# A gated linear attention and a spatial-gating MLP on one core: units in another order, and shifted due times for 66 steps beside TensorE

## The chip, the cores and the metric

The kernel runs on one core of one Trainium2 chip. The metric is the device time of one execution in microseconds (us). The kernel before took 347.85 us (median of 3 runs, 346.72 to 348.61). Engines: PE is TensorE (matmuls), PEld its weight loads, DVE VectorE, ACT ScalarE, POOL GpSimd; SP issues the DMAs.

## What is computed

Cut to what matters:

```python
# attention: batch 4, 8 heads, 768 steps, head dimension 48
for t in range(S):
    state = alpha[:, :, t, :, None] * state + einsum('bhd,bhe->bhde', k[:, :, t], v[:, :, t])
    y[:, :, t] = einsum('bhd,bhde->bhe', q[:, :, t], state)
x = y.transpose(0, 2, 1, 3).reshape(B, S, H * D)          # (4, 768, 384)
# MLP with a spatial gate
h = gelu(x @ w_in)                                         # 384 -> 1024
u, v = h[..., :512], h[..., 512:]
v_n = (v - mean) / sqrt(var + 1e-6) * g_ln
v_s = einsum('ts,bsd->btd', w_sg, v_n) + b_sg[None, :, None]
out = x + (u * v_s) @ w_out
```

## The kernel before

**Chunks.** The recurrence is cut into 24 chunks of 128 steps, six for each of the four batches, numbered 0 to 23. A scan on DVE (line 415) makes the running product of the decays of a chunk, a second scan (437) its inverse; k and q are scaled with them (428, 444), and the rest of a chunk is small matmuls of 64x64, run two at a time in the two halves of the array ("tiled").

**Units of PE.** The program for PE is a sequence of units, written out by hand in the string `ORDER`. `S i`, `A i`, `M i`, `H i` are the four tiled units of chunk i: scores (line 472), their product with v and the gains of the state (487, 510), the second half of that with the carried state (487, 498), the end (498). `T i` transposes k for the first chunks. `V b c` (mm_v, 9 matmuls of 128x512) and `U b h d` (mm_u, 9 of 128x384) are the products with w_in, `P b h d` (mm_s, 18) the spatial product, `R b h k` (mm_o, 12) that with w_out. `Q g m` (mm_q, 9) are the pieces of the spatial product of the last batch, which is computed with seven products in place of eight from sums of weights and values. Every float32 matmul that needs precision is three matmuls of high and low halves (lines 703 to 705).

**Around a chunk.** `A i` waits for the masked scores (`causal`, DVE, line 581) and for the rows of k (`kn`, ACT, 614 and 618). Between `A i` and `M i` stands `turn`, a tiny write that orders the two halves of a bank: on POOL a memset of `relay`, on ACT a copy of `alo` (line 554). `H i` waits for `half` (633, DVE or ACT). After `H i` ACT copies y out (`xf` 659, `y3` 649), SP packs it with two DMAs (662), ACT rounds it (`xh`, 670), DVE takes the rest (`xl`, 674). `V` needs `xh` and `xl`; its output goes through GELU, moments, the root on POOL (730, 731), the normalisation and again a split into `vh` (ACT 747) and `vl` (DVE 751), which `P` reads in the order of the six chunks.

**Sums of weights.** `weight_sums` (854) makes the four sums of blocks of w_sg for the last batch: six loads of 393 KB, 12 differences (872), 12 roundings on ACT (876), 12 remainders (880), 24 stores to DRAM (883). Its loads may start at the planner's time `SUMS`; 24 `fetch` DMAs (899) bring the sums back later.

**The planner.** Everything on the other engines is a step with an engine, a cost, predecessors and buffers. `Plan.dues` (97) gives each step a due time, worked back from the due times of the units; `Plan.issue` (122) then walks through a modelled time and at each point takes, among the steps of an engine that could start nearly at once, the one with the lowest `order`:

```python
near = [x for x in c if x[0] - left[x[2]]["keen"] <= t0 + (150 if e == "pe" else 60)]
t, way_order, n, way = min(near, key=lambda x: x[1])
```

What it picks is written into the program in that order, so each engine and SP's queue run strictly in it. Where a step has two possible engines, the walk takes the one that would end it first.

**The branch.** Near the end all engines load a count (`cnt_i`, line 1588) and branch (1589): a slow path is skipped when the inputs are in range. A hint for the branch is given to PE alone, behind the last but one `Q` of `ORDER` (`hint_at`, 1122).

Of the kernel before, what the change touches and what calls it, by code (L numbers as in the profile page):

```python
# [48 lines left out]
F64_MIN_AS_F32 = float(np.array(0x38100000, np.uint32).view(np.float32))  # L49

ORDER = """
    T0 A0 H0 S0 A1 S1 M0 T2 T1 S2 T3 H1 V00 S3 V01 M1 H2 M2 A2 S4 U000 A3 M4 H3 U002 M3 T4 A4 S5 T5 A5 V02 S6 M5 H4
    V03 S7 M6 H5 A7 H6 A6 V04 V05 U001 U010 P000 S8 P002 M7 U013 U003 U011 P003 P001 S9 P010 P013 H7 A8 S10 H8 H9 M8
    A9 U012 R000 M9 R001 V11 V10 P012 R002 A10 P011 S11 V12 A11 S12 H10 M11 M10 U100 H11 R011 A12 M12 U103 V13 R012
    P101 P100 V14 R010 V15 U101 P103 U102 H12 S13 P102 U111 U112 R102 U113 S14 U110 M13 S15 A13 H14 H13 A14 P110 M14
    R100 P112 U203 R101 P113 S16 A16 H15 A15 P111 V22 M15 M16 H16 U202 R111 V24 V23 R112 R110 S18 M17 S17 A18 V21 A17
    U200 H17 M18 H18 V20 S19 S20 A19 U201 M20 A20 M19 H19 V25 S21 H20 P200 U210 P202 P210 U211 R202 P203 A21 P201 S22
    R200 P211 P213 R201 H21 M21 V31 S23 A22 H22 U213 M23 V30 M22 H23 A23 P212 V34 U212 V35 V32 U310 U302 U303 Q11 Q12
    R211 Q01 V33 R212 R210 U312 Q02 Q05 U300 U301 U311 Q06 Q04 Q16 Q17 Q15 Q03 Q07 R301 U313 Q13 R310 Q14 R311 C0 R302
    R300 R312  # L60
"""

FIRST = (
    ("a", 0), ("kqv", 0), ("ws", 0), ("ws", 1), ("v", 0), ("a", 1), ("kqv", 1), ("wv", 0), ("v", 1), ("wv", 1),
    ("ws", 2), ("ws", 3), ("ws", 4), ("ws", 5),
)


class Plan:
# [27 lines left out]
    def dues(self):  # L97
        kids = {n: [] for n in self.steps}
        for n, s in self.steps.items():
            for a in s["after"]:  # L100
                kids[a].append(n)
        memo = {}

        def due(n):
            if n in memo:
                return memo[n]
            s = self.steps[n]
            memo[n] = 1e9
            d = s["due"] if s["due"] is not None else 1e9
            if s["soon"] is not None:  # L110
                a, ns = s["soon"]
                d = min(d, due(a) + ns)
            cost = s["ns"] + (s["reach"] or self.REACH[s["eng"]]) + (2200 + round(s["nbytes"] / self.RATE) if s["nbytes"] else 0)
            for k in kids[n]:
                d = min(d, due(k) - cost - self.steps[k]["lead"].get(n, 0))
            memo[n] = d
            return d

        for n in self.steps:
            self.steps[n]["order"] = due(n)  # L120

    def issue(self, units, ahead):
        self.dues()
# [71 lines left out]
def tile_gla_gmlp(ctx: ExitStack, tc: tile.TileContext, aT, kqv, w_in, w_sgT, w_out, g_ln, b_sg, out):  # L195
# [903 lines left out]
    n = B * NCH  # L1099
# [23 lines left out]
    due = {}  # L1123
# [10 lines left out]
    for name, p in pieces:  # L1134
        def at(k, name=name):
            return (k,) + name
# [188 lines left out]
    for b in range(B):  # L1325
        for c in range(NCH):
            summed = b in SUMMED
            st_ = mlp_v(xs.setdefault((b, c // CPH), {}), vns[b][c], c, summed)
            v = ("V", b, c)
# [18 lines left out]
        for hf in range(2):  # L1348
            x = xs[b, hf]
# [52 lines left out]


    LAST = ("V", B - 1, NCH - 1)
    SUMS = 140000.0
    order = (0, 1, 3, 2)
    for k in range(NK):
        load, total, high, low_half, keep = weight_sums(k)
# [5 lines left out]
        for w in range(2):  # L1414
            plan.add(at("load", w), "sp", 330, lambda w=w, load=load: load(w), takes=[("raw", 2, uses[w])], nbytes=393216, start=SUMS)
        for m, (prev, users) in zip(order, ((None, [at("t", 1)]), (0, [at("t", 3)]), (1, []), (3, []))):
# [127 lines left out]
    for k, src in enumerate(words):  # L1544
        t = {}

        def load(src=src, t=t):
            t["raw"] = stage.tile([P, TH, 2], I32, tag="raw", name="raw", bufs=2)
            nc.sync.dma_start(t["raw"], src.bitcast(I32).rearrange("p (n two) -> p n two", two=2))
# [127 lines left out]
```

## Time and profile before

| | before |
|---|---|
| time, median of 3 runs | 347.85 us (346.72 to 348.61) |
| time of the profiled execution | 347.15 us |
| its span, first to last instruction | 345.4 us |
| granted TensorE clock, mean | 0.993 |
| PE busy | 333.7 us, 97% |
| PEld busy | 301.1 us, 87% |
| DVE busy | 264.4 us, 77% |
| ACT busy | 186.8 us, 54% |
| POOL busy | 60.2 us, 17% |

The span is the time between the first and the last instruction on the core; the 1.75 us between it and the execution's own time lie around it. Busy time of PE counts a matmul from its start to its modelled end, and matmuls overlap: what a unit costs is therefore read here from the start of its first matmul to the start of the next unit's first.

### The profile page before, as it was taken

How to read it: one execution, taken by the hardware profiler on the slowest of the kernel's cores; microseconds unless marked ns; L12 is line 12 of the kernel's file. 1: busy time of each engine (PE TensorE's matmuls, PEld its weight loads, DVE VectorE, ACT ScalarE, POOL GpSimd, SP SyncE). 2: the span in 40 equal slices, each digit the busy share in tenths (PEclk: the TensorE clock that was granted, in tenths of full speed). 3: DMA queues.
4: the chain of work that ended last, by engine and by line, in shares of the span. 5: the costliest groups of instructions: out<-in, count | busy, mean ns of one | idle time of the engine just before them, and what ended most of it. 6: DMA issues, size and time to landing. Idle time of an engine off the chain costs nothing. (4 is left out here: it accounts for less than half of the span.)

```text
span 345.4 us, 10871 instructions
## 1 busy us (share of the span) xinstructions
PE 333.7 (97%) x4435; PEld 301.1 (87%) x4435; DVE 264.4 (77%) x547; ACT 186.8 (54%) x462; POOL 60.2 (17%) x145
## 2 busy tenths in 40 slices
PE   8989999899999999999999998998999999999996
PEld 4667888699979988999999986897999899999996
DVE  5999997799998786488679787868655576896752
ACT  4656887988354788545546466759322445241210
POOL 2011313241022324100010034530000124000000
PEclk9999999999999999999999998999999999999999
DMA  7968676658535462646776676897981340010012
GB/s 246 376 203 248 207 181 198 179 122 245 163 103 155 105 183 63 180 149 174 237 184 185 205 207 199 297 267 92 384 272 49 88 137 0 25 46 2 6 58 86
DMA packets 45227, 56.17 MB, mean 163 GB/s; under 512 B 18800, under 2 KB 38384, under 8 KB 45168
## 3 DMA queue, kind: packets, MB, share of 16 engines
q1 hardware_dynamic: 45168, 55.39, 54.1%
q8 instruction: 36, 0.59, 0.7%
q14 instruction: 23, 0.19, 0.2%
HBM read 38.84 MB, written 9.44 MB: 140 GB/s over the span
## 5 line engine op out<-in xcount | busy, mean ns | idle before, releaser
L703 PE MATMUL mm_s<-ws_hi,vh 128*128 128x384 f32 x144 | 48.8, 339 | 0.8 <-ACT vh L747 0.6
L705 PE MATMUL mm_s<-ws_hi,vl 128*128 128x384 f32 x144 | 48.3, 335 | 0.1
L704 PE MATMUL mm_s<-ws_lo,vh 128*128 128x384 f32 x144 | 48.1, 334 | 0.0
L703 PE MATMUL mm_u<-xh,wi_hi 128*128 128x384 f32 x96 | 33.0, 344 | 0.0
L705 PE MATMUL mm_u<-xh,wi_lo 128*128 128x384 f32 x96 | 32.2, 336 | 0.0
L704 PE MATMUL mm_u<-xl,wi_hi 128*128 128x384 f32 x96 | 32.2, 335 | 0.0
L703 PE MATMUL mm_v<-wi_hi,xh 128*128 128x512 f32 x72 | 29.8, 414 | 0.7 <-ACT xh L670 0.7
L840 ACT CAST gh<-g 128x384 fp32r<-128x384 f32 x28 | 14.2, 512 | 27.6 <-DVE g L837 16.1
L704 PE MATMUL mm_v<-wi_lo,xh 128*128 128x512 f32 x72 | 28.7, 399 | 0.0
L705 PE MATMUL mm_v<-wi_hi,xl 128*128 128x512 f32 x72 | 28.7, 399 | 0.0
L703 PEld LDWEIGHTS mm_s<-ws_hi,vh 128*128 128x128 f32 x144 | 27.0, 188 | 1.8 <-ACT vh L747 0.9
L703 PE MATMUL mm_o<-gh,wo_hi 128*128 128x384 f32 x84 | 28.3, 337 | 0.0
L705 PE MATMUL mm_o<-gh,wo_lo 128*128 128x384 f32 x84 | 28.1, 335 | 0.0
L704 PE MATMUL mm_o<-gl,wo_hi 128*128 128x384 f32 x84 | 28.1, 334 | 0.0
L705 PEld LDWEIGHTS mm_s<-ws_hi,vl 128*128 128x128 f32 x144 | 27.0, 188 | 0.4 <-DVE vl L751 0.4
L704 PEld LDWEIGHTS mm_s<-ws_lo,vh 128*128 128x128 f32 x144 | 27.0, 188 | 0.0
L487 PEld LDWEIGHTS y<-at,kqv_t 64*64 64x64 f32 x768 | 16.1, 133 | 11.7 <-issue 5.1
L487 PE MATMUL y<-at,kqv_t 64*64 64x64 f32 x768 | 22.1, 227 | 3.6 <-POOL relay L554 1.3
L415 DVE TENSOR_TENSOR_SCAN pf<-a,floor 128x387 f32<-128x387 f32 x24 | 22.8, 955 | 2.7 <-DMA a<-in_aT 2.5
L614 ACT COPY kn<-kt 128x768 uint16<-128x768 uint16 x18 | 19.2, 1068 | 9.0 <-PE dl L510 5.4
L424 POOL COPY pend<-pf 128x3 f32<-128x3 f32 x24 | 10.1, 421 | 78.3 <-DVE pf L415 70.9
L1004 DVE TENSOR_TENSOR r<-mm_o,xf 128x384 f32<-128x384 f32 x23 | 12.5, 552 | 14.1 <-PE mm_o L705 11.0
(198 smaller groups left out, 876.0 us busy)
## 6 DMA issues: line engine op xcount, KB each, us to landing
kqv_t<-in_kqv SPq DMA_DIRECT2D x22, 586.0 KB, 4.3
a<-in_aT SPq DMA_DIRECT2D x30, 194.0 KB, 3.8
raw<-in_w_in SPq DMA_DIRECT2D x14, 384.0 KB, 4.9
out_x<-r SPq DMA_DIRECT2D x23, 192.0 KB, 2.1
raw<-in_w_out SPq DMA_DIRECT2D x8, 384.0 KB, 4.2
sum_t<-t_dram SPq DMA_DIRECT2D x16, 192.0 KB, 4.6
kqv_t<-kqv_t SPq DMA_DIRECT2D x48, 48.2 KB, 2.9
raw<-in_w_sgT SPq DMA_DIRECT2D x6, 384.0 KB, 4.4
```

Of the source, the lines that this page charges most:

```text
L415: nc.vector.tensor_tensor_scan(pf.rearrange("p j t -> p (j t)"), s["a"][:, 0:NK * C1], floor.rearrange("p j t -> p (j t)"), initial=0.0, o ...
L424: nc.gpsimd.tensor_copy(pend[:, i], st[i]["pf"][:, :, C])
L487: lambda j=j: nc.tensor.matmul(y_of(y, m, j, e)[:, half(h)], v[half(h), D * (2 * j + e):D * (2 * j + e) + 64], at[half(h), e, m, j], start ...
L614: nc.scalar.copy(to[:, 0:2 * NK * P].rearrange("t (k d two) -> t two k d", two=2, k=NK), kt,)
L703: nc.tensor.matmul(o, lh, rh, start=(idx == 0 and not onto), stop=False, skip_group_check=shared)
L704: nc.tensor.matmul(o, lh, rl, start=False, stop=False, skip_group_check=shared)
L705: nc.tensor.matmul(o, ll, rh, start=False, stop=(idx == n - 1), skip_group_check=shared)
L840: nc.scalar.copy(gate_part(g, "h", d), t["g"])
L1004: nc.vector.tensor_tensor(t["r"], t["o"], x["xf"][:, kk], op=ALU.add)
```

## The change

Three things change, and no step is added or taken away. `ORDER` lists the same 221 units in another sequence. A new table `SHIFT` adds an amount in ns to the `order` of 66 steps that are not on PE; the walk then picks those steps earlier or later among their rivals. And `SUMS` goes from 140000 to 95000, so the sums of weights may be loaded earlier. As the lines move down by 15, line 554 is 569 in the changed kernel, 880 is 895, and so on.

```diff
 ORDER = """
-    T0 A0 H0 S0 A1 S1 M0 T2 T1 S2 T3 H1 V00 S3 V01 M1 H2 M2 A2 S4 U000 A3 M4 H3 U002 M3 T4 A4 S5 T5 A5 V02 S6 M5 H4
...
+    M0 S1 T0 S0 A0 H1 M1 T1 A1 H0 T3 V00 S2 T2 S3 V01 A3 A2 M2 H2 S4 U000 U002 A4 H3 M3 S5 T4 M4 A5 T5 H4 V02 V03 A6
...
 """
+SHIFT = """
+    load_wv_1:68663 power_wv_2:-1890 power_wu_2:-12837 load_wu_3:-6539 rest_wu_3:-20747 load_ws_2_0:64246
...
+"""
...
+        shift = {n: int(v) for n, v in (x.split(":") for x in SHIFT.split())}
         for n in self.steps:
-            self.steps[n]["order"] = due(n)
+            self.steps[n]["order"] = due(n) + shift.pop("_".join(map(str, n)), 0)
+        assert not shift, shift
...
-    SUMS = 140000.0
+    SUMS = 95000.0
```

**What it moves on PE.** The sequence written for PE passes between tiled units and full-size ones 58 times before and 52 times in the change. Gone are three islands of tiled units between large ones: `H7 S9`, `H12 S13`, and `S17` between `R112` and `R110`; one is new (`H13 S14`, seven large units behind `M13`). Near the start `S2 T2` now stands behind `M1 H1`, not ahead of them. The last `V` is `V32` where it was `V33`. The hint for the branch stands 73 matmuls ahead of it, where it stood 45 ahead.

**POOL around chunk 17.** The first fence is of before, the second of the change. `rstd` and `off` belong to a unit `V` of batch 2 (moments `mv`), `pend` to the scan of a later chunk, and the memset of `relay` is `turn` of chunk 17, for which `M17` waits.

```order
L730 TENSOR_SCALAR rstd_3482<-mv_3475 128x1
L731 TENSOR_TENSOR rstd_3482<-rstd_3482,nhalf_106 128x1
L735 TENSOR_SCALAR off_3525<-mv_3475,rstd_3482 128x1
L880 TENSOR_TENSOR sum_lo_3529<-sum_w_3349,sum_hi_3480 128x384
L730 TENSOR_SCALAR rstd_3536<-mv_3532 128x1
L731 TENSOR_TENSOR rstd_3536<-rstd_3536,nhalf_106 128x1
L554 MEMSET relay_105 128x1
L735 TENSOR_SCALAR off_3579<-mv_3532,rstd_3536 128x1
```

```order
L745 TENSOR_SCALAR rstd_3442<-mv_3438 128x1
L746 TENSOR_TENSOR rstd_3442<-rstd_3442,nhalf_106 128x1
L750 TENSOR_SCALAR off_3451<-mv_3438,rstd_3442 128x1
L745 TENSOR_SCALAR rstd_3470<-mv_3453 128x1
L746 TENSOR_TENSOR rstd_3470<-rstd_3470,nhalf_106 128x1
L750 TENSOR_SCALAR off_3496<-mv_3453,rstd_3470 128x1
L439 COPY pend_109<-pf_3521 128x3
L569 MEMSET relay_105 128x1
L745 TENSOR_SCALAR rstd_3626<-mv_3614 128x1
```

Before, the root of `V24` (730, 731) and a remainder of the sums (880) stand right ahead of the memset; in the change it stands behind the root and the offset of the earlier `V23` and one copy, the next root comes after it, and the sum is no longer on POOL.

**ACT around chunk 14.** `turn` of chunk 14 was on POOL right behind that of chunk 13. In the change it is the copy of `alo` on ACT:

```order
L891 CAST sum_hi_2947<-sum_w_2871 128x384
L436 COPY kqv_t_2920<-pf_2489 128x3
L619 COPY pi_2534<-kqv_t_2920 128x768
L685 CAST xh_2836<-xf_2621 128x3x128
L819 ACTIVATE u_3025<-mm_u_2977 128x384
L569 COPY alo2_88<-alo_98 128x1
L891 CAST sum_hi_3047<-sum_w_2945 128x384
```

Ahead of it now stand the decay's end and the planes of chunk 17 (436, 619), `xh` of chunk 13 (685), which waits for two DMAs, and the GELU of `U112` (819), the unit right before `A14`.

**DVE ahead of chunk 10.** The first fence is of before, the second of the change; the last row of each is `half` of chunk 10 (`s_m<-s_c,dl0`), for which `H10` waits.

```order
L1004 TENSOR_TENSOR r_1999<-mm_o_1948,xf_393 128x384
L437 SCALAR_TENSOR_TENSOR pi_2003<-a_1633,ends_103 128x387
L415 SCALAR_TENSOR_TENSOR pf_2027<-a_1993,floor_100 128x387
L432 RECIPROCAL ends_103<-pf_2027 128x3
L1004 TENSOR_TENSOR r_2054<-mm_o_2012,xf_393 128x384
L843 TENSOR_TENSOR gl_2056<-g_1713,gh_2052 128x384
L832 SCALAR_TENSOR_TENSOR g_2063<-mm_s_1973,g_col_119,b_bc_120 128x384
L843 TENSOR_TENSOR gl_2056<-g_1764,gh_2052 128x384
L837 TENSOR_TENSOR g_2063<-g_2063,u_1827 128x384
L437 SCALAR_TENSOR_TENSOR pi_2068<-a_1993,ends_103 128x387
L832 SCALAR_TENSOR_TENSOR g_2100<-mm_s_2033,g_col_119,b_bc_120 128x384
L633 TENSOR_TENSOR s_m_111<-s_c_110,dl0_2080 112x192
```

```order
L1019 TENSOR_TENSOR r_2017<-mm_o_1937,xf_401 128x384
L430 SCALAR_TENSOR_TENSOR pf_2022<-a_1984,floor_100 128x387
L895 TENSOR_TENSOR sum_lo_2047<-sum_w_1986,sum_hi_2024 128x384
L447 RECIPROCAL ends_103<-pf_2022 128x3
L887 TENSOR_TENSOR sum_w_2054<-raw_1905,sum_w_1997 128x384
L858 TENSOR_TENSOR gl_2059<-g_1706,gh_2049 128x384
L1019 TENSOR_TENSOR r_2061<-mm_o_2004,xf_401 128x384
L847 SCALAR_TENSOR_TENSOR g_2063<-mm_s_1964,g_col_119,b_bc_120 128x384
L858 TENSOR_TENSOR gl_2059<-g_1774,gh_2049 128x384
L452 SCALAR_TENSOR_TENSOR pi_2070<-a_1984,ends_103 128x387
L648 TENSOR_TENSOR s_m_111<-s_c_110,dl0_2082 112x192
```

Two steps of the sums (880 as 895, 872 as 887) have come in between the scans and the outputs; they are the third and fourth of the 24, and before, the first of them stood 38 rows behind this `half`. In the walk's order the sums now lie beside the units `P012` to `P113`, where they lay beside `P100` to `V20`; 23 of the 24 are on DVE in both.

## Rows read from the trace of the kernel before

**Rows 1.** The page, part 1: busy time, share of the span, instructions of each engine.

```profile
PE 333.7 (97%) x4435; PEld 301.1 (87%) x4435; DVE 264.4 (77%) x547; ACT 186.8 (54%) x462; POOL 60.2 (17%) x145
```

**Rows 2.** Busy time by stretch: us; PE, PEld, DVE, ACT, POOL; granted clock; DMA share; GB/s.

```profile
20.00:40.00 20.00, 18.85 (x459) 14.40 (x451) 19.07 (x44) 13.39 (x39) 5.00 (x11) 1.00 0.68 209
...
80.00:100.00 20.00, 19.61 (x353) 18.42 (x351) 19.39 (x44) 11.31 (x28) 2.06 (x4) 1.00 0.67 193
100.00:120.00 20.00, 19.76 (x225) 18.54 (x226) 17.10 (x35) 11.04 (x28) 4.92 (x11) 1.00 0.43 118
...
200.00:220.00 20.00, 18.54 (x316) 15.93 (x315) 15.96 (x32) 13.75 (x33) 8.56 (x14) 0.91 0.71 213
```

**Rows 3.** Timeline of PE, chunks 10 and 17: start, us, operation, [idle before <- releaser].

```profile
117.30 0.46 PE L487 MATMUL y<-at,kqv_t 64*64 64x64 f32 x16
118.04 0.65 PE L472 MATMUL sc<-kqv_t 48*64 48x64 f32 x30
118.47 0.45 PE L487 MATMUL y<-at,kqv_t 64*64 64x64 f32 x16
...
121.57 0.46 PE L487 MATMUL y<-at,kqv_t 64*64 64x64 f32 x16
...
208.28 0.46 PE L487 MATMUL y<-at,kqv_t 64*64 64x64 f32 x16
...
210.97 0.55 PE L487 MATMUL y<-at,kqv_t 64*64 64x64 f32 x16 [1.31 <-POOL relay L554]
...
212.31 0.79 PE L703 MATMUL mm_v<-wi_hi,xh 128*128 128x512 f32 x1
...
215.64 0.46 PE L487 MATMUL y<-at,kqv_t 64*64 64x64 f32 x16
```

**Rows 4.** Timeline of POOL in the same place.

```profile
209.50 1.37 POOL L731 TENSOR_TENSOR rstd<-rstd,nhalf 128x1 f32<-128x1 f32 x1
210.82 0.10 POOL L554 MEMSET relay<- 128x1 f32 x1
```

**Rows 5.** Timeline of PE, first matmuls of four spatial products of batch 2.

```profile
230.83 0.34 PE L703 MATMUL mm_s<-ws_hi,vh 128*128 128x384 f32 x1
...
235.63 0.44 PE L703 MATMUL mm_s<-ws_hi,vh 128*128 128x384 f32 x1 [0.29 <-DVE s_c L641]
...
238.87 0.33 PE L703 MATMUL mm_s<-ws_hi,vh 128*128 128x384 f32 x1
...
241.99 0.33 PE L703 MATMUL mm_s<-ws_hi,vh 128*128 128x384 f32 x1
```

**Rows 6.** Timeline of ACT in that stretch.

```profile
233.08 0.51 ACT L670 CAST xh<-xf 128x384 fp32r<-128x384 f32 x1 [1.19 <-DMA xf<-y]
233.50 0.61 ACT L747 CAST vh<-vg 128x512 fp32r<-128x512 f32 x1
```

**Rows 7.** Timeline of PE, `M12`.

```profile
128.80 0.46 PE L487 MATMUL y<-at,kqv_t 64*64 64x64 f32 x16 [0.47 <-ACT alo L554]
```

**Rows 8.** Timeline of PE around `S17`: last matmul of `R112`, first two of `R110`.

```profile
204.88 0.34 PE L705 MATMUL mm_o<-gh,wo_lo 128*128 128x384 f32 x1
...
205.77 0.45 PE L703 MATMUL mm_o<-gh,wo_hi 128*128 128x384 f32 x1
206.05 0.34 PE L704 MATMUL mm_o<-gl,wo_hi 128*128 128x384 f32 x1
```

**Rows 9.** Timeline of PE, `A7`.

```profile
65.93 0.46 PE L487 MATMUL y<-at,kqv_t 64*64 64x64 f32 x16 [0.91 <-ACT y L649]
```

**Rows 10.** A group of instructions: count | busy, mean ns of one | idle before.

```profile
L880 DVE TENSOR_TENSOR sum_lo<-sum_w,sum_hi 128x384 fp32r<-128x384 f32 x11 | 6.0, 545 | 2.2 <-DMA t_dram<-sum_lo 2.2
```

**Rows 11.** Waits of ACT: us in total, times, longest.

```profile
ACT xh L670 <- DMA xf<-y: 6.5, 6, 2.2
```

**Rows 12.** Timeline of PE and of DVE at the branch.

```profile
335.20 0.33 PE L703 MATMUL mm_h<-gates,wo_hi 128*128 128x192 f32 x1 [0.37 <-PEq L1589]
...
334.21 1.49 DVE L1004 TENSOR_TENSOR r<-mm_o,xf 128x384 f32<-128x384 f32 x3 [3.03 <-DVEq L1589]
```

More of the change, by code (lines that the diff above doesn't have):

```diff
@@ L51 @@
 ORDER = """
-    T0 A0 H0 S0 A1 S1 M0 T2 T1 S2 T3 H1 V00 S3 V01 M1 H2 M2 A2 S4 U000 A3 M4 H3 U002 M3 T4 A4 S5 T5 A5 V02 S6 M5 H4
[L53 to L60, printed above, removed]
+    M0 S1 T0 S0 A0 H1 M1 T1 A1 H0 T3 V00 S2 T2 S3 V01 A3 A2 M2 H2 S4 U000 U002 A4 H3 M3 S5 T4 M4 A5 T5 H4 V02 V03 A6
+    M6 S6 H5 M5 A7 S7 V05 H6 U001 V04 S8 P001 H7 U010 M7 P000 U003 U013 P003 P002 P010 P013 S9 A8 H8 S10 A9 H9 R002 M8
+    V10 V11 M9 U011 R001 P012 R000 P011 A10 M10 U100 S11 U012 H10 S12 M11 R012 A11 H11 V14 V12 A12 V13 U102 H12 M12
+    R010 S13 R011 P102 M13 V15 U110 P100 U103 A13 U113 R101 P103 P101 P110 U101 R100 S14 P112 H13 U112 S15 A14 M14 M15
+    R102 H15 A15 H14 S16 P111 P113 U111 H16 R111 M16 S17 A16 V23 V22 R112 U202 V21 A17 S18 V24 H17 R110 S19 M17 H18
+    S20 A19 A18 M18 H19 V20 U200 U201 M19 V25 P201 S21 M20 U211 H20 A20 P200 R201 U203 P202 P203 U213 U212 R202 S22
+    A21 H21 R200 A22 P213 S23 M21 U210 M23 H22 A23 P210 M22 V30 V31 P211 H23 P212 V33 R211 V34 V35 V32 U302 R210 U303
+    U312 Q12 Q11 R212 U310 U301 Q02 Q01 Q15 U300 Q07 Q17 Q14 Q04 Q06 Q16 Q13 U311 Q05 R300 Q03 R301 U313 R310 R302 C0
+    R311 R312
 """
@@ L66 @@
 )
+SHIFT = """
+    load_wv_1:68663 power_wv_2:-1890 power_wu_2:-12837 load_wu_3:-6539 rest_wu_3:-20747 load_ws_2_0:64246
+    load_ws_4_0:25080 load_wo_0:6902 load_wo_1:2976 sign_wo_1:7087 rest_wo_1:1049 load_wo_2:7862 sign_wo_2:7048
+    sign_wo_3:-8013 load_ws_1_1:-6730 low_ws_1_1:-11126 load_ws_2_1:-14921 load_ws_3_1:51 v_0:104280 pair_0_1:-22062
+    xf_0:4635 kqv_1:101851 v_1:98852 pair_1_1:-2733 state_1:10677 causal_2:4002 state_2:-21529 pack_2_0:3939 k_3:57944
+    xh_3:12788 scan_4:24016 end_4:3345 y3_4:1598 pack_4_0:4583 xl_4:-11262 q_5:2240 end_5:2808 pend_6:3746 q_7:-1199
+    causal_7:-7421 pack_7_0:3896 kqv_8:3084 xl_8:12929 k_9:-515 scan_10:-3263 q_10:-4937 causal_10:1677 state_10:16564
+    xh_10:19413 end_11:33197 k_12:-3679 scan_13:-3225 q_14:5240 pack_14_1:-1526 q_15:-8058 xf_15:16449 xl_16:7065
+    q_17:554 causal_20:12087 planes_22:1156 V_0_2_8:-10949 V_0_3_6:6430 P_0_0_1_1:31350 P_0_0_2_4:-3727
+    P_0_0_3_4:-9151 P_0_1_0_1:-4453 P_1_1_3_4:-16293 V_2_3_5:-7554 V_2_4_8:-37313 U_3_1_3_1:4581
+"""
 class Plan:
```

## The prediction

> **What bounds the kernel now.** I read the page's busy times first, then the stretches, then the timeline of PE unit by unit, and last, at each place where PE lost time, the timelines of the engines it waited for. By the first, PE is busy for 97% of the span [rows 1], and nothing else comes near; only 11.7 us of 345.4 show it idle. That understates what it loses. A busy matmul is counted to its modelled end, and a late clock or a half-filled pipeline is counted as busy too. So I take each unit from the start of its first matmul to the start of the next unit's first and compare it with another unit of the same kind. The reader is to see in rows 3 how much that changes. Chunk 10 with the `V` behind it runs from 117.30 to 121.57, 4.27 us for A, S, M, H and V. The same five units of chunk 17 run from 208.28 to 215.64, 7.36 us. The wait that the row itself shows is 1.31 us; the whole loss is 3.09 us, since PE's clock fell while it waited: the granted clock of that stretch is 0.91 where the others have 1.00 [rows 2], so part of it ran at 1.2 GHz and not at 2.4, and the nine matmuls of `V21` take 3.33 us, from 212.31 to 215.64 [rows 3].
>
> So the kernel is bound by PE's own sequence plus the few places where the strict order of another engine keeps PE waiting. In the first 60 us or so these are waits on DVE, which from 20 to 40 us is busy for 19.07 of 20 [rows 2]; later they are single accidents in the order of a queue.
>
> **What the change removes, part by part.**
>
> *The wait at `M17`.* The memset that releases it came at 210.82, right behind a root on POOL that took 1.37 us from 209.50 [rows 4] and a remainder of the sums ahead of that. In the change the memset stands behind the root of the `V` before and a copy that depends on a scan alone; `V24`, whose root was in the way, comes after chunk 17 on PE. The cover is a large unit: `V21` now runs between that root and `A17`. I take the whole loss as gone: 3.09 us.
>
> *The wait inside `P200`.* It runs from 230.83 to 235.63, 4.80 us, where `P201`, from 238.87 to 241.99, needs 3.12 [rows 5]: 1.68 us lost. What it lacked was `vh` of `V25`, made on ACT at 233.50, right behind a rounding `xh` that had itself held ACT up for 1.19 us until a DMA of packed rows landed [rows 6]. In the change no `xh` stands between the normalisation of `V25` and its `vh`, and the bulk of the sums' loads, stores and first fetches, which shared the DMA engines with these packs, has been issued some 28 to 35 us of PE's work earlier. `P` starts as soon after `V25` as before, so the cover is no larger, only the queue shorter. I take 1.68 us.
>
> *The wait at `M12`.* ACT wrote `alo` late by 0.47 us [rows 7], behind the planes of chunk 14. In the change this release is on POOL, behind a root that begins one large unit ahead of `A12`: 0.47 us gone.
>
> *Islands.* From the last matmul of `R112` to the first of `R110` it is 0.89 us, and 0.28 to the next [rows 8], where matmuls of one unit follow each other by 0.17 (3.12 us for the 18 of `P201` [rows 5]). `S17` between them thus cost 0.72 and 0.11, together 0.83; inside a tiled block an S costs 0.43, from 118.04 to 118.47 [rows 3]. An island costs 0.40 us, then. Three go and one comes: 0.80 us less. The fourth, `S2 T2` near the start, I count at nothing: its cover is DVE, which is late there whatever PE does, and without that cover it would be 0.40 more.
>
> Gone in all: 3.09 + 1.68 + 0.47 + 0.80 = 6.04 us.
>
> **What it adds.** *Earlier sums.* Six of the 24 steps on DVE now stand ahead of chunk 12, where DVE has 0.6 us free of the stretch from 80 to 100 and 2.9 of the next [rows 2]. One such step is 0.545 us [rows 10]. If each stood right ahead of a step that PE waits for, all six would be felt: 3.3 us. If all fall in DVE's free time, none is. Less than nothing I exclude, because the time they free at their old place is already in the terms above. Four of them fall into the stretch that has 2.9 us free, so I take the nearer end, one step's worth: 0.6 us. *A longer queue at `A7`.* PE waited 0.91 us there for the copy `y3` on ACT [rows 9]; in the order of ACT one more rounding stands ahead of that copy, of the size of the 0.51 us one in [rows 6]. ACT has no gap there, so it is felt nearly in full; the bounds are 0 and 0.5, and I take 0.5. *`turn` of chunk 14 on ACT.* Behind `xh` of chunk 13 it can be held up by a late pack. Waits of that kind come six times in the trace, 6.5 us together, and the longest is 2.2 [rows 11]. But `R100`, `P112` and `U112` run between `H13` and `A14`, 39 matmuls at 0.17 us [rows 5], 6.8 us as a cover. Bounds 0 and 2.2; with that much cover I stay near the lower end, 0.3.
>
> Everything else on PE is the same work in another sequence. At the end the first `Q` that needs sums of values stands twelve units behind the last `V`, in both orders; I count that at nothing, its cover being those twelve units, and if DVE were late there, `Q15` would wait first.
>
> **The sum.** -6.04 + 0.6 + 0.5 + 0.3 = -4.64 us. The profiled execution took 347.15 us around its span of 345.4 and would take 342.5; it lies 0.7 below the median of the runs shown, 347.85, and against that the change comes to **343.2 us**.
>
> **The rivals.**
>
> *B: the branch.* PE waits 0.37 us at the branch and DVE, which is given no hint, 3.03 [rows 12]. The hint now comes 73 matmuls ahead of it and not 45. If what the hint brings in is no longer there when PE arrives, PE pays what DVE pays: 2.66 us more, 345.9 us. For it speaks that nothing in the trace shows a hint as far ahead; against it, that the hint worked at 45. The Trainium skill, "Runtime: NRT & Kernel Launch", section "Instruction fetch mechanics", says that a taken branch to a target outside the window of two pages has to fetch before it goes on; by that rule alone a hint that is spent too soon would cost as in this rival, and no run before shows it.
>
> *C: the accident comes back elsewhere.* The order is again one that was fitted to modelled times, and the old one was too. `A14` with its `turn` on ACT, `A16` with the same behind `xh` of chunk 15, or the release of chunk 20 behind the root of `V25` could be the new `M17`: a wait of over a microsecond, and the clock falls. Then 3.09 us of the gain is given back: 346.3 us. For it speaks that the trace of before has several such places, one of them that large; against it, that I find more PE work ahead of these than there was at `M17`.
>
> *D: DVE becomes the bound from chunk 9 to chunk 11, and the kernel is slower.* There DVE is busy for 19.39 of 20 us already [rows 2], the splits of w_out are packed closer together, and the sums come on top. `S9` now comes right ahead of `M8`, so that only M, H and one `V`, 3.10 us as from 118.47 to 121.57 [rows 3], cover the mask of chunk 9. The point that decides is whether DVE is further behind than those 3.1 us when `S9` ends. If it is, `A9`, `A10` and `A11` each begin late, and each time PE may lose what it lost at chunk 17: two of them cost 6.2 us and give 349.4, three cost 9.3 and give 352.5. Against it: the six steps are 3.3 us in all [rows 10] and there is nearly as much free time behind.
>
> **How the numbers follow.** The forecast gets 0.64, B 0.08, C 0.18, D 0.10. A measurement can tell about 0.5% from no change, 1.7 us here: faster is below 346.1, slower above 349.6. The forecast lies below in all its bounds but the worst; half of B and 0.05 of C do too: 0.73. The rest of B and C is no change, 0.17; D is slower, 0.10. The range: with none of the added costs it is 347.85 - 6.04 = 341.8, and the fastest run shown lies 1.1 below its median, so it begins at 340.7. Upwards it takes in B, and C with the 0.8 by which the slowest run exceeds the median: 347.1. Left out are D and little more.
>
> **What would show it right or wrong.** Right: no wait of PE on POOL's `relay` near a microsecond, a granted clock of 1.00 in the stretch of chunks 16 to 19, `P201` (now the first of batch 2) in 3.1 to 3.3 us, `M12` without a wait, and PE's start of the last unit 4 to 5 us earlier, with the first 65 us within 0.5 us of before. Wrong: a wait of PE at the branch of some 3 us (B), a wait over 1 us at `M14`, `M16` or `M20` with the clock down behind it (C), DVE without a gap and PE waiting for `at` or for the state between 95 and 125 us (D). If the 65 us at the start have changed by more than 1 us, my view of DVE as the bound there is wrong, on either side.

## The result, and the profile after

The changed kernel takes 350.09 us (median of 22 executions, 347.61 to 354.49). Beside it the kernel before took 345.81 (22 executions, 343.89 to 349.28), 2.0 us less than the three runs that the prediction started from. The ratio is 1.0109, with a 95% interval of 1.0080 to 1.0137: slower by some 4 us, where 4.6 us less was forecast. The profiled execution took 353.83 us and is one of the slowest of its kernel; I rest only on what other profiles of the same order show too.

The page of the changed kernel, first its span, then PE's busy time and the granted clock in 40 slices:

```profile
span 352.1 us, 10871 instructions
PE 335.6 (95%) x4435; PEld 304.0 (86%) x4435; DVE 263.4 (75%) x545; ACT 187.4 (53%) x463; POOL 60.2 (17%) x146
PEclk9999699999987999999999999999999999999999
```

The work is the same as in [rows 1]; PE is idle 4.8 us more. The clock falls in two places that had none before, and the one of [rows 2] at 200 to 220 us is gone. The same in the stretches of the kernel after:

```profile
20.00:40.00 20.00, 16.14 (x295) 11.92 (x294) 15.89 (x36) 10.54 (x31) 4.51 (x8) 0.86 0.59 171
80.00:100.00 20.00, 19.82 (x174) 19.25 (x176) 18.06 (x39) 13.32 (x32) 0.72 (x3) 1.00 0.68 158
100.00:120.00 20.00, 17.28 (x263) 15.19 (x253) 16.93 (x37) 7.56 (x21) 3.93 (x6) 0.83 0.59 166
200.00:220.00 20.00, 19.84 (x317) 17.44 (x316) 16.75 (x35) 15.05 (x37) 5.04 (x12) 1.00 0.67 178
```

What I had set out to remove is gone. PE's timeline of the kernel after at `A7`, at `M12`, at `A17`, `M17` and `V24`, and at the first and second product of batch 2 (`P201`, `P200`):

```profile
72.73 0.46 PE L502 MATMUL y<-at,kqv_t 64*64 64x64 f32 x16 [1.52 <-ACT y L664]
...
142.25 0.45 PE L502 MATMUL y<-at,kqv_t 64*64 64x64 f32 x16
...
215.22 0.46 PE L502 MATMUL y<-at,kqv_t 64*64 64x64 f32 x16
...
216.54 0.46 PE L502 MATMUL y<-at,kqv_t 64*64 64x64 f32 x16
...
217.38 0.50 PE L718 MATMUL mm_v<-wi_hi,xh 128*128 128x512 f32 x1
...
236.22 0.44 PE L718 MATMUL mm_s<-ws_hi,vh 128*128 128x384 f32 x1
...
239.45 0.33 PE L718 MATMUL mm_s<-ws_hi,vh 128*128 128x384 f32 x1
```

`M17` waits for nothing [rows 3], nor does `M12` [rows 7], and `P201` takes 3.23 us where the first P of batch 2 took 4.80 [rows 5]. `A7` waits 1.52 us, 0.61 more than in [rows 9]. The new loss is at chunk 8. Here PE's timeline there and the stretch behind it:

```profile
100.43 0.44 PE L513 MATMUL y<-kqv_t,s_c 48*48 48x64 f32 x16
103.60 0.68 PE L513 MATMUL y<-kqv_t,s_m 48*48 48x64 f32 x16 [2.72 <-DVE s_m L648]
104.21 0.80 PE L718 MATMUL mm_v<-wi_hi,xh 128*128 128x512 f32 x1
...
108.35 0.71 PE L502 MATMUL y<-at,kqv_t 64*64 64x64 f32 x16
```

```profile
103.00:109.00 6.00, 5.40 (x50) 3.93 (x54) 4.33 (x11) 1.80 (x6) 1.79 (x1) 0.50 0.49 167
```

`H8` waits 2.72 us for `half` of chunk 8 on DVE (the expectations below call this the wait at M8, since it lies in M8's stretch). PE had been without a gap of 0.2 us since `A7`; while it waits, at 102.80, its clock falls to 0.50, that is 1.2 GHz, and the nine matmuls of `V10` take 4.14 us (104.21 to 108.35) where `V11` in the same trace takes 2.18. Together with slow `H8` and `A9` that is 5.5 us lost in one place.

**Where DVE lost the time.** Between the halves of chunks 7 and 8 DVE has 27.5 us of work in 28.1 in the kernel before, and 25.9 us in the kernel after, where PE needs 26.3 between `A7` and `A8`. Neither has slack. Waits of DVE in that stretch, first before, then after (us in total, times, longest; the two waits for `dl` are those of the halves themselves):

```profile
DVE s_m L633 <- PE dl L510: 1.0, 2, 0.9
DVE g L832 <- PE mm_s L705: 0.3, 1, 0.3
```

```profile
DVE kqv_t L443 <- ACT pi L619: 1.6, 1, 1.6
DVE kqv_t L459 <- DMA kqv_t<-in_kqv: 1.2, 1, 1.2
DVE s_m L648 <- PE dl L525: 0.8, 1, 0.8
DVE ws_lo L288 <- ACT ws_hi L285: 0.7, 1, 0.7
```

DVE's row of the half of chunk 8, after:

```profile
103.20 0.34 DVE L648 TENSOR_TENSOR s_m<-s_c,dl 112x192 f32<-112x192 f32 x1
```

So it stood idle for 3.6 us on the way, and came 3.4 us late to the half (`S9`, right behind `A8`, begins at 99.77, the half at 103.20). The 1.6 us come from ACT, the 1.2 from SP. The timelines of ACT and of SP's queue after:

```profile
78.21 0.82 ACT L753 ACTIVATE vg<-vg,off,rstd 128x512 f32<-128x512 f32 x1 [1.22 <-POOL off L790]
78.93 0.83 ACT L619 COPY pi<-kqv_t 128x768 uint16<-128x768 uint16 x1
```

```profile
79.79 1.25 SPq L623 DMA_TRANSPOSE kt<-pi  x1
...
86.94 0.38 SPq L422 DMA_DIRECT2D kqv_t<-in_kqv  x1
```

The normalisation of `V05` was on DVE before; in the change it is on ACT, waits there for an offset from POOL, and the planes of chunk 9 stand behind it. SP's queue has their transposition, and behind that, ten issues later, the load of chunk 11, which DVE asks for early.

### The profile page after: what moved, and what is told of

Its sections match the earlier page's. It is cut to its first block, busy times and chain, and to the rows that moved or that the text cites. A ratio compares the mean times of both kernels' runs of the same rounds, so it can differ in the third digit from the quotient of the medians.

```text
span 352.1 us, 10871 instructions
## 1 busy us (share of the span) xinstructions
PE 335.6 (95%) x4435; PEld 304.0 (86%) x4435; DVE 263.4 (75%) x545; ACT 187.4 (53%) x463; POOL 60.2 (17%) x146
## 5 line engine op out<-in xcount | busy, mean ns | idle before, releaser
L720 PE MATMUL mm_o<-gh,wo_lo 128*128 128x384 f32 x84 | 28.1, 335 | 0.0
L719 PE MATMUL mm_o<-gl,wo_hi 128*128 128x384 f32 x84 | 28.1, 335 | 0.0
L452 DVE TENSOR_TENSOR_SCAN pi<-a,ends 128x387 f32<-128x387 f32 x24 | 22.9, 956 | 3.4 <-DMA kt<-pi 3.2
L439 POOL COPY pend<-pf 128x3 f32<-128x3 f32 x24 | 8.3, 349 | 89.5 <-DVE pf L430 89.3
L847 DVE SCALAR_TENSOR_TENSOR g<-mm_s,g_col,b_bc 128x384 f32<-128x384 f32 x24 | 14.7, 612 | 10.9 <-PE mm_s L720 10.9
```

The costliest lines, as they stand in the source:

```text
L439: nc.gpsimd.tensor_copy(pend[:, i], st[i]["pf"][:, :, C])
L452: nc.vector.tensor_tensor_scan(pi.rearrange("p j t -> p (j t)")[:, ::-1], s["a"][:, NK * C1:0:-1], ends.rearrange("p j t -> p (j t)")[:, : ...
L719: nc.tensor.matmul(o, lh, rl, start=False, stop=False, skip_group_check=shared)
L720: nc.tensor.matmul(o, ll, rh, start=False, stop=(idx == n - 1), skip_group_check=shared)
L847: nc.vector.scalar_tensor_tensor(t["g"], t["o"], g_col[:, d:d + 1], b_bc[:, tsl], op0=ALU.mult, op1=ALU.add,)
```

## The experiments

**Is it the same in every execution?** The changed kernel and the kernel before, unchanged, each with a second profile.

> The changed kernel as it is, for a second profile. In the first one TensorE paused for 1.46, 2.34 and 0.74 us with nothing to wait for, each time at record 705, 961 and 6593 of its own instruction stream (193 + a multiple of 256), 2.3 to 2.5 us after a 16 KB instruction fetch had begun. Theory 'instruction pages': the pauses come back at these same three records, each over 0.5 us, and behind the second the clock falls again. Rival 'chance' (a DMA that happened to be late): at most one of the three comes back. Theory 'DVE late at chunk 8': M8 waits 2 to 3 us for its state's half and the clock falls again; by chance it would be under 1 us.

Measured: 350.73 us, ratio 1.0134 (1.0062 to 1.0205). `H8` waits 3.10 us, and the clock falls again; PE pauses at records 705 (1.46) and 961 (2.06; pauses at records are counted from the start of the record ahead), not at 6593. The wait at chunk 8 belongs to the order.

> The kernel before as it is, for a second profile. The prediction took 3.09 us at M17 (a wait for POOL's memset, behind a root of 1.37 us, and the clock's fall) and 1.68 us inside P200 as losses that every execution has. Theory 'one-off': M17 waits under 0.5 us, the root in front of the memset takes 0.5 to 0.7 us, the clock does not fall there, and the first P of batch 2 takes under 4 us. Theory of the prediction, 'every execution': M17 waits over 1 us and the clock falls behind it. Theory 'instruction pages': TensorE pauses again at records 705 (H1) and 3265 (H9), 0.6 to 1 us each.

Measured: one execution of 345.82 us. POOL's and PE's timelines at `M17` in it, then ACT's in front of `P200`:

```profile
209.97 0.57 POOL L731 TENSOR_TENSOR rstd<-rstd,nhalf 128x1 f32<-128x1 f32 x1
210.48 0.10 POOL L554 MEMSET relay<- 128x1 f32 x1
```

```profile
209.20 0.46 PE L487 MATMUL y<-at,kqv_t 64*64 64x64 f32 x16
...
210.64 0.46 PE L487 MATMUL y<-at,kqv_t 64*64 64x64 f32 x16
...
213.76 0.46 PE L487 MATMUL y<-at,kqv_t 64*64 64x64 f32 x16
```

```profile
231.84 0.51 ACT L670 CAST xh<-xf 128x384 fp32r<-128x384 f32 x1 [1.26 <-DMA xf<-y]
232.25 0.61 ACT L747 CAST vh<-vg 128x512 fp32r<-128x512 f32 x1
```

The root that took 1.37 us in [rows 4] takes 0.57, and chunk 17 with its `V` runs from 209.20 to 213.76, 4.56 us in place of 7.36: 0.29 over the clean 4.27. The 3.09 us were a one-off. The wait inside `P200` is there again, 1.88 us in all, and `A12` loses 0.68: those two belong to the order.

**Is the order of VectorE at the half to blame?**

```diff
+for w in (("rest", "wo", 1), ("rest", "wo", 3), ("power", "wo", 1), ("sub", "wo", 1)):
+    plan.steps[w]["after"].append(("half", 8))
```

> The changed kernel in which four steps of the splits of w_out on VectorE may not go before the half-state of chunk 8 (in the changed kernel they stand right ahead of it). Theory 'DVE late at chunk 8': M8 waits under 1 us, the clock stays at 1.00 from 100 to 110 us, and the time is 3 to 5 us less, 345 to 347 us; if it is the sum of VectorE's work that binds and not its order there, the wait moves to the first R, 1 to 3 us, and the time is only 0 to 3 us less. Rival 'instruction pages alone': the wait at M8 did not matter, the same within 1 us.

Measured: 358.46 us, ratio 1.0333 (1.0236 to 1.0431). `H8` still waits 2.48 us, and the first R waits for `wo_lo`, 2.9 us in two waits. But the run is muddled: one more predecessor makes the walk choose anew, and 98 of DVE's 539 picks moved, 49 on ACT, 53 on SP. From here on the picks of the changed kernel are played back from a written list, so that one row moves and all others stay.

```diff
 # DVE
-power_wo_1 sub_wo_1 rest_wo_3 rest_wo_1 low_wo_3 low_wo_1
 P_0_1_0_1 half_8
+power_wo_1 sub_wo_1 rest_wo_3 rest_wo_1 low_wo_3 low_wo_1
```

> The changed kernel with six steps of the splits of w_out moved on VectorE from right ahead of the half-state of chunk 8 to right behind it, some 3 us of work; nothing else moves on any engine. Theory 'order at M8': M8 waits under 0.8 us and the time is 3 to 5 us less. Theory 'VectorE is behind with all that the first R needs' (the chain theory, too, since the idle time is upstream): M8 waits less, the first R waits 2 to 4 us instead, and the time is within 2 us of the changed kernel's.

Measured: 349.95 us, ratio 1.0146 (1.0093 to 1.0198). `H8` waits 0.71 us, and 2.3 us stand at the mask of chunk 9 (`A9`) instead. The wait is only passed on, though not to the first R, as I had expected: what is late is DVE as a whole.

**Or the two late inputs?** One swap on ACT (run `r_p9`):

```diff
 L633 COPY kn<-kt 128x96 x2
-L753 ACTIVATE vg<-vg,off,rstd 128x512
 L619 COPY pi<-kqv_t 128x768
+L753 ACTIVATE vg<-vg,off,rstd 128x512
```

> The changed kernel with one swap on ScalarE and nothing else moved on any engine: the planes of chunk 9 go ahead of the normalisation of V05, which in the changed kernel stands in front of them and waits about 1.2 us for an offset from POOL. Theory 'late at chunk 8 by a chain': VectorE stood idle for 3.6 to 4.1 us between the half-states of chunks 7 and 8 in four profiles of the changed order (0.4 and 0.8 in two of the old order), 1.6 of it for these planes and most of the rest for loads that SP issues behind the transposition of the same planes. Then VectorE's idle time there falls below 2.2 us, M8 waits under 1.3 us, the clock stays at 1.00 there, and the time is 3 to 5 us less than the changed kernel's 350 us. Rival 'too much work on VectorE': its sum of work binds; M8 waits less, but the first R waits instead, 1.5 to 3 us, and the time is at most 2.5 us less. Rival 'loads on their own': SP's loads are late for another reason, VectorE's idle time falls by the 1.6 us alone and M8 still waits 1.3 to 2 us.

Measured: 349.02 us, ratio 1.0142 (1.0080 to 1.0205). DVE's waits ahead of the half, and PE at `H8`:

```profile
DVE kqv_t L459 <- DMA kqv_t<-in_kqv: 1.5, 1, 1.5
DVE s_m L648 <- PE dl L525: 0.8, 1, 0.8
DVE vl L766 <- ACT vh L762: 0.6, 1, 0.6
DVE top L326 <- DMA raw<-in_w_out: 0.4, 1, 0.4
```

```profile
99.12 0.44 PE L513 MATMUL y<-kqv_t,s_m 48*48 48x64 f32 x16 [1.98 <-DVE s_m L648]
```

The 1.6 us are gone, DVE meets the late load instead, `H8` waits 1.98 us, and the clock falls all the same (0.68 from 99 to 103 us). The rival "loads on their own" had this. So the load goes forward too (run `r_p9k`):

```diff
 L463 DMA kqv_t<-kqv_t 48x1x257 x2
+L422 DMA kqv_t<-in_kqv 128x1172
 L677 DMA xf<-y_1456 16x3x128 x2
...
 L282 DMA raw<-in_w_sgT 128x384
-L422 DMA kqv_t<-in_kqv 128x1172
 L623 DMA_TRANSPOSE kt<-pi 128x6x128
```

> The swap of r_p9 and one more move: SP issues the load of chunk 11's k, q and v right behind the pairs of chunk 9, six issues earlier (about 4.4 us); nothing else moves. In r_p9 VectorE still stood idle for 2.6 us ahead of the half-state of chunk 8, 1.45 of it for this load, and M8 still waited 2.2 us. Theory 'chain of late inputs to VectorE': its idle time there falls to about 1 us, M8 waits under 1 us, the clock stays at 1.00 behind it, and the time is 2.5 to 4.5 us less than r_p9's 349.0 us, 344.5 to 346.5. Rival 'too much work on VectorE': the wait moves to the first R, 1 us or more, and the time is less by at most 1.5 us.

Measured: 345.06 us, ratio 0.9998 (0.9965 to 1.0030). The same two views:

```profile
DVE s_m L648 <- PE dl L525: 0.8, 1, 0.8
DVE vl L766 <- ACT vh L762: 0.6, 1, 0.6
DVE ws_lo L288 <- ACT ws_hi L285: 0.5, 1, 0.5
```

```profile
96.62 0.44 PE L513 MATMUL y<-kqv_t,s_m 48*48 48x64 f32 x16 [0.53 <-DVE s_m L648]
```

Two moved rows, none on TensorE, give the whole slowdown back. The missing fourth, the load alone (run `r_k`):

> The changed kernel with the earlier load of chunk 11 alone, without the swap on ScalarE. In r_p9 (the swap alone) the ratio to before stayed at 1.0142; with both it fell to 0.9998. If the load is the cause and the swap idle, the ratio is 0.996 to 1.004 and M8 waits under 1 us. If both are needed (VectorE is late by the planes' 1.6 us or by the load's, whichever is left), M8 still waits 1.2 to 2.2 us with the clock falling behind it, and the ratio is 1.006 to 1.015.

Measured: 346.14 us, ratio 1.0018 (0.9978 to 1.0057). DVE waits the 1.6 us for the planes, `H8` waits

```profile
98.19 0.44 PE L513 MATMUL y<-kqv_t,s_m 48*48 48x64 f32 x16 [1.42 <-DVE s_m L648]
```

and the clock stays at 1.00 from 98 to 102 us. My expectation for this wait was right and that for the time wrong. In these two profiles the clock fell with 1.98 us and not with 1.42. The granted clock of every execution is on record as a mean over its span: it is 0.995 or less in all 22 of the change and all 4 with the swap, in 8 of 12 with the load, in 2 of 10 with both moves and in 6 of 25 of the kernel before beside them. By these means the change lacks 3.5 us of full clock on average and the version with both moves 0.8, so that some 2.7 us of what the moves give back (3.8 by the ratios) is clock; this is an estimate from above, since for part of that time PE stood still. The load decides; the swap alone shows no gain in the median, and beside the load it is worth 0.7 us by the ratios, which is within the intervals.

The length of a wait alone does not say whether the clock falls. It fell with `M17`'s 1.31 us before, and it did not with 2.27 us at `A9` in the run with the six steps moved, nor with 2.15 us at `H16` in a run further below (`r_all64`). PE's rows and the stretches behind them, in that order:

```profile
103.67 0.46 PE L502 MATMUL y<-at,kqv_t 64*64 64x64 f32 x16 [2.27 <-DVE at L596]
103.00:109.00 6.00, 4.67 (x139) 4.01 (x140) 5.90 (x16) 2.97 (x8) 1.67 (x2) 1.00 0.71 225
```

```profile
197.56 0.44 PE L513 MATMUL y<-kqv_t,s_m 48*48 48x64 f32 x16 [2.15 <-DVE s_m L648]
198.00:203.00 5.00, 5.00 (x24) 4.27 (x24) 4.60 (x11) 3.80 (x11) 0.44 (x3) 1.00 0.62 146
```

**Which part of the change makes it?** `SHIFT`, whose table has 70 entries and not 66, emptied, `ORDER` and `SUMS` kept:

> The new order of units and the earlier sums, without the table of shifts; the planner then chooses the order on the other engines anew, with the normalisation of V05 on VectorE. If the shifts make the wait at chunk 8, M8 waits under 1 us and the time is 2 to 4 us less than the changed kernel's (346 to 348 us). If the order of units makes it (1.8 us less TensorE work ahead of chunk 8 than before), M8 or the first R waits 2 us or more all the same, and the time is 349 us or more. The pauses at records 705 and 961 stay in any case where the same units stand there.

Measured: 362.52 us (354.62 to 364.82). The list that the walk then makes loses in many places (`H` units wait for `s_m` 4.3 us in four waits, the first `P` 2.8 for `u`), so the run does not isolate chunk 8. It shows that order and shifts are one fitted thing: this order needs its shifts.

**The other rivals: M16, and pauses with nothing to wait for.** In six of nine profiles with `turn` of chunk 16 on ACT, `M16` waited 0.7 to 2.0 us for it, as rival C had it for this chunk. ACT in `r_p9k` stood there in front of chunk 19's decay:

```profile
191.84 0.20 ACT L436 COPY kqv_t<-pf 128x3 f32<-128x3 f32 x1 [3.58 <-DMA kqv_t<-in_kqv]
```

The next run (`r_all64`) puts that turn on POOL; it starts from `r_p9k_page64`, the two moves with PE's stream shifted, which follows below.

> As r_p9k_page64, with the turn of chunk 16 on POOL as in the kernel before; nothing else moves. On ScalarE it stands behind a copy that waits for a DMA, and M16 waited 0.4 to 2.2 us for it in five of six profiles of the changed order, the longest time with the clock falling behind it. If that is the cause (rival C of the prediction, at A16), M16 waits under 0.3 us in the profile and the time is 0.5 to 2 us less than r_p9k_page64's. If another step of ScalarE or POOL is late there, M16 still waits and the time is the same within 0.7 us.

Measured: 344.69 us, ratio 0.9982 (0.9942 to 1.0022). The turn came in time, and `H16` waited 2.15 us for its half on DVE, which had waited behind k of the same chunk 19. So both stand behind one load (run `r_m16`):

```diff
 # ACT                          # DVE
-pend_19                       -k_19 q_19
 turn_16                        half_16
+pend_19                       +k_19 q_19
```

> The two moves of r_p9k and one more: on ScalarE and VectorE the steps of chunk 19 (decay's end, k, q, planes) go behind the turn and the half-state of chunk 16, in front of which they wait 3.5 us for a load. Nothing moves on TensorE, POOL or SP. Theory 'late load in front of M16': M16 waits under 0.3 us in the profile (1.0 to 2.3 us in r_p9k, r_p9k_page64 and r_all64, whichever engine made its turn), and the time is 0.5 to 2 us less than r_p9k's, ratio to the kernel before 0.993 to 0.999. Rival 'something else is next': M17 or A18 takes over the wait, and the ratio stays within 0.003 of r_p9k's 0.9998.

Measured: 344.87 us, ratio 0.9986 (0.9953 to 1.0018). No wait at `M16` or `H16` in the profile; instead `M17` waits 0.40 us for its turn on POOL, behind a copy that waits for a scan on DVE, and `A19` 0.42 for a copy on ACT. That fits the rival "something else is next": the ratio is within 0.003 of that of `r_p9k`.

The pauses: PE's timeline of the kernel after in `H2`, where 14 of 16 matmuls run and the rest come late, with no releaser:

```profile
32.74 0.43 PE L513 MATMUL y<-kqv_t,s_m 48*48 48x64 f32 x14
35.30 0.34 PE L513 MATMUL y<-kqv_t,s_m 48*48 48x64 f32 x1 [2.13 <-issue]
```

Behind it the clock was low in this execution, and a second pause, of 1.46 us, stood between `S2` and `T2`:

```profile
35.00:41.00 6.00, 5.70 (x43) 4.25 (x44) 4.34 (x9) 2.02 (x5) 0.00 (x0) 0.50 0.63 173
```

A further 32 keep-warm matmuls, where PE waits for its first weights, move all later instructions by 64:

```diff
-GAP, SHORT = 14, 22
+GAP, SHORT = 12, 56
```

> The changed kernel with 32 more keep-warm matmuls at the start (two of 384 columns fewer, 34 of 64 columns more), in a place where TensorE waits for a DMA: every later instruction of TensorE moves by 64 in its stream, so the page borders move 64 records toward the start of the program. Theory 'instruction pages': no pause over 0.5 us is left behind S2 and within H2; pauses may come 64 records earlier (in H1 and M2), and the time moves by 2 us or more, most likely down, to 345 to 348 us. Rival 'the place itself' (these units wait for something else): the pauses stay behind S2 and in H2, and the time is the same within 1 us, 349 to 351 us. 'DVE late at chunk 8' expects the wait at M8 unchanged, 2 to 3 us.

Measured: 348.43 us, ratio 1.0073 (1.0037 to 1.0108). Behind `S2` and in `H2` PE no longer pauses without a releaser. It pauses at records 3777, 6593 and 7105 of the shifted stream, 1.15, 0.76 and 1.56 us: in `U100` (this one the profile puts down to `vg` on DVE), `A19` and `P201`, not in `H1` and `M2` as I had thought. `H8` waits 2.83 us, as before.

> The kernel before with the same 32 more keep-warm matmuls. Theory 'instruction pages': its pauses of 0.85 and 0.84 us at H1 and H9 (records 705 and 3265) leave these units and come, if at all, 64 records earlier; the time is within 2 us of before, in either direction. Rival 'the place itself': they stay at H1 and H9 and the time is the same within 0.5 us.

Measured: 345.63 us, ratio 1.0031 (0.9993 to 1.0069). The pauses in `H1` and `H9` are gone, one of 0.94 us stands at record 7105 (`H20`). In this profile too the root ahead of `M17` takes 0.57 us and `M17` does not wait.

The swap of `r_p9` with this shift:

> The same swap, and the 64 further TensorE instructions at the start that moved the page borders off S2 and H2 (3.0 to 7 us less TensorE loss up to chunk 4 in the trace, 2.3 us less in the median). If the two causes are separate, their gains add up: 343 to 346 us, within 0.5% of the kernel before or faster. If they are one (the pauses at S2 and H2 make VectorE late), it is no faster than the better of the two alone, 347 us or more.

Measured: 349.33 us, ratio 1.0127 (1.0070 to 1.0184); `H8` still waits 2.31 us, and `M16` 1.96. It is no faster than the swap alone or the shift alone.

Both moves of `r_p9k` with it:

> The same two moves with the page borders moved by 64 instructions. If the pauses at S2 and H2 cost what the traces show and are not replaced, it is 1.5 to 4 us faster than r_p9k, 341 to 344.5 us; if the pauses at U100 and P201 that took their place in the two runs with this border, and M16's wait, eat it, it is within 1 us of r_p9k.

Measured: 344.92 us, ratio 1.0009 (0.9967 to 1.0052), no pause of 0.5 us at any border in the profiled execution.

And `r_m16` with it:

> The same with the page borders of TensorE's stream moved by 64 instructions. If the pauses at S2 and H2 are worth what the profiles show net of those at U100, M19 and P201, it is 0.5 to 2 us faster than r_m16, ratio 0.988 to 0.996; if they only change places, the two are within 1 us.

Measured: 344.41 us, ratio 0.9976 (0.9946 to 1.0006), the best of all versions: 1.3% less than the ratio of the change, and not to be told from the kernel before. In its profile `M17` waits 0.76 us for the turn on POOL and `M16` 0.39. Five pairs with and without the shift of 64 show no sign of a steady gain in the median (1.0134 and 1.0073, 1.0142 and 1.0127, 0.9998 and 1.0009, 0.9986 and 0.9976, and 1.0031 for the kernel before): the pauses move with the borders, and what they cost in the median stays open; no pair differs by more than 0.6%.

## Why the prediction was wrong, by its steps

**The wait at `M17`, 3.09 us: the step that failed on the side of the gain.** It took a loss of one execution for one of every execution. Three profiles of the kernel before have one long root there and two of 0.57 us; what the order lost in the second profile is 0.3 us. (The clock, too, fell not while PE waited, as the prediction has it, but 0.24 us after `M17` had started, at 211.21.) The prediction's own condition, that the loss is set by a root of 1.37 us, was the hint: 0.57 us is the median of the 24 roots of that trace.

**Rival D, given 0.10: the step that failed on the side of the loss.** PE did wait for the state on DVE, and the clock fell; but DVE was not "without a gap", as D's sign has it, for it stood idle 3.6 us ahead of the half. The place was one chunk earlier, and the price 5.5 us in one place, not 3.1 in each of two. (That the median is near D's 349.4 owes something to chance: the base was 2.0 too high, and 2.8 of the gain in it did not exist.) The argument against D added up DVE's work and its free time. It left out what DVE waits for: it has no slack in the 28 us ahead of chunk 8, and there a step that changed from DVE to ACT, and a load in SP's queue, cost it 2.8 of those 3.6 us. I had read ACT's order at chunk 14 and DVE's at chunk 10, and neither ACT's nor SP's at chunk 9. The early sums were not tried alone; with them in place the two moves give the slowdown back.

**The base.** 347.85 was the median of three; of 22 it is 345.81. That alone moved the forecast by 2 us.

**The rest of the sum.** `P200` (1.68) and `M12` (0.47) were right and went as forecast. `A7` was put at 0.5 and measured 0.61. `M14` shows no wait (0.3 was taken). The islands (0.80) were not measured alone. Rival B fell: PE waits 0.30 us at the branch, 0.37 before [rows 12]. Rival C came at `A16`, at 0.7 to 2.0 us in most profiles, with the clock falling at `M16` in one of them. That the first 65 us would stay within 0.5 us was wrong, though not because of DVE: PE's own pauses behind `S2` and in `H2` were in no step of the prediction, and where the shift of 64 takes them away `A7` begins at 66.97 us in the change and at 66.04 in the kernel before. The gains that held, some 2.5 us with `P200`, `M12` and what `M17` cost in the second profile, do not show in the time: without the loss at chunk 8 the change comes to a ratio of 0.9998. These pauses, `A7` and `M16` are the losses seen that could pay for them; that they do so in the median is not shown.

## What to carry to other kernels

A wait in one profile is a gain only if its releaser is always that late: compare the releaser's duration with its like in the same trace, or take a second profile, before it goes into a sum. Where an engine's work fills the stretch in which PE needs its result, don't count its instructions alone: follow the queue of each engine and of SP that feeds it, row by row, in the new order; two rows there were worth more than all reordering of TensorE. And what a wait of PE costs depends on whether the clock falls with it, which its length did not tell here: look at the granted clock behind the wait, and at that of every execution.

## What was not expected of the hardware

The pauses of PE with "issue" as their cause sit at fixed places of its instruction stream. The page of the kernel after counts the fetches:

```profile
q8 instruction: 36, 0.59, 0.7%
```

These are 36 fetches of 16 KB for 8919 records of PE (4435 matmuls, as many weight loads, and 49 of its sequencer), one for some 250. Counted through 17 profiles of all kernels here, 35 gaps of 0.5 us or more, from the start of one record to the next, stand exactly at records 193 + a multiple of 256, and for 32 of them a fetch of this queue had begun 2.2 to 3.0 us earlier. In none of the 578 crossings did PE go on sooner than 2.16 us after the start of the fetch. Between large units, where a record stands for 0.09 us, the fetch begins up to 28 us ahead and costs nothing; tiled units run through 256 records in as little as 2.0 us, and if it begins late there, PE stands. Why it began in front of the border by 0 records in one place and by nearly 300 in another was not found. The Trainium skill, "Runtime: NRT & Kernel Launch", section "Instruction fetch mechanics", says that instructions come in blocks of 16 KB (256 instructions) and that crossing into the next is mostly hidden. The size agrees with these counts, and so does "mostly", since 543 of 578 crossings show no gap of 0.5 us; most of those that do lie in tiled units.
